# Delta rule and gated MLP on one core: GpSimd's tensor_tensor replaced, zero products tied to the first solve, weight loads paced, new ranks

## Chip, cores, metric

One core of a Trainium2 chip. The metric is the device time of one execution in microseconds, less is better.

## What is computed

The reference runs a delta rule over 4 x 8 heads of 768 steps with head size 48, and puts its output through an MLP with w_in (384 x 2048) and w_out (2048 x 384), both float64 in memory:

```
k_n = k / (norm(k) + 1e-06)
for t in range(S):
    y[t] = einsum('bhd,bhde->bhe', q[t], state)
    v_old = einsum('bhde,bhd->bhe', state, k_n[t])
    state = state + beta[t] * einsum('bhd,bhe->bhde', k_n[t], v[t] - v_old)
x = y.transpose(0, 2, 1, 3).reshape(B * S, H * D)
h = x @ w_in
g = h * tanh(log1p(exp(h)))
out = g @ w_out
```

## The kernel before

The 768 steps are cut into 12 chunks of 64 steps. All 32 heads of a chunk are worked on together. Within a chunk the recurrence is a triangular system. Its solution is made for two chunks at a time, in a group g (`early`, L496): k is turned (kt), products pg give the inner products of k, `diagonal` and `beside` (L534, L539) bring the blocks out of PSUM, `first_block` (L548) masks one of them on GpSimd, VectorE transposes (gt, L564), normalizes (L577 to L604) and eliminates column by column (`step`, L638, the pairs of lines L643 and L644). For the first two groups the elimination is of 16 columns, and `merge` (L676) joins the halves by products ma (L686) and mb (L697), an addition (L702) and a transpose tn (L705). Products ta and tb (`s_a2`, `s_b2`) complete the inverse.

A chunk then goes through `s_gq` (products of k and the state with k and q), `s_z` (pz), `s_y` (py for the output, ps for the new state), each for two halves h of the heads. `turn` (L1017) transposes the output into x, as a high and a low part. v is scaled by the norms first (`scale_v`, L866: eight ScalarE instructions a half for chunk 0, one GpSimd tensor_tensor a half after that, L876), and gq waits for it.

`moe(n)` (L1036) is the MLP on the 256 rows of chunk n, in eight steps fp: up (h, 18 products), Mish and a cast on ScalarE (L1070, L1071), a subtraction for the low part (L1073, on VectorE, but on GpSimd for steps 6 to 15 counted from the start, by GP0 = 6), and down (acc, 12 products).

The weights come as pairs of 32-bit words, 28 pieces (`parts`: three of w_in, four of w_out, four times over). `load_w` issues their loads on SP, one after another. `convert` (L391) makes two float32 parts of each: a copy on ScalarE (L415), a clamp (L426, on GpSimd or, for every fourth piece, on VectorE), a sign (L423 on GpSimd or L421 on VectorE), two joins on VectorE (L430), the high part on ScalarE (L442), and the low part by products with an identity (loi, loo, L447 and L449) for the first 25 pieces.

The order of every engine's instructions is made while the program is built: `Plan` keeps a list of operations with an engine, a cost and a priority, and runs them in a simulated time; the constants SOON to GQ2 near the end are these ranks. The planner also models how TensorE's instructions arrive (`feed`). Where it finds TensorE idle during the first 220 us it puts in products of zeros (`fill_up`, L101, `fill`, L479), which write to a spare PSUM tile named warm.

## Time and profile before

| what | us |
|---|---|
| median of three runs | 639.32 (639.23 to 641.89) |
| the profiled execution | 637.26 |
| its span | 635.5 |
| TensorE busy | 605.9 (95%) |
| VectorE busy | 447.7 (70%) |
| ScalarE busy | 277.3 (44%) |
| GpSimd busy | 157.3 (25%) |

Busy time is an average over very different stretches: the first solve, the conversion of the weights with the first chunk, the second solve, and a steady stretch from there to the end. The span is the profiled execution's from its first to its last instruction; 1.8 us of its time lie around it.

### The profile page before, as it was taken

Reading aid. Unit: us, or ns where it says so; the run is one execution under the profiler, and the core shown is the slowest. Engines: PE = TensorE matmul, PEld = TensorE weight load, DVE = VectorE, ACT = ScalarE, POOL = GpSimd, SP = SyncE. Lnnn points to the kernel's source line nnn. Section 1 sums busy time; section 2 is a strip of 40 time slices with the busy share of each in tenths; the row PEclk is TensorE's granted clock in tenths of the full one; section 3 lists DMA queues with packets and bytes.
Section 4 is the critical chain, followed back from the end, with each engine's and each line's share of the span. In section 5 each row is a group of like instructions: output and inputs, shape, how many; then the busy total and the mean of one; then the engine's idle time right before and its main releaser. Section 6 shows DMA issues by size and latency. Waiting matters only on the chain.

```text
span 635.5 us, 21881 instructions
## 1 busy us (share of the span) xinstructions
PE 605.9 (95%) x9536; PEld 552.8 (87%) x9536; DVE 447.7 (70%) x954; ACT 277.3 (44%) x602; POOL 157.3 (25%) x156
## 2 busy tenths in 40 slices
PE   6888999995899999999999999999999999999997
PEld 3446787894899999999999999999999999999997
DVE  4856889998147999587999569996789994631110
ACT  1725887531354333545224643236543326443331
POOL 5494779751314110103111012101031110000000
PEclk9878999996899999999999999999999999999999
DMA  7997342001324121342213351105131220110011
GB/s 109 387 399 122 53 64 53 2 1 36 44 38 68 39 39 27 51 76 37 45 24 51 44 85 40 26 14 77 34 47 38 40 44 10 27 27 1 1 26 25
DMA packets 156256, 37.70 MB, mean 59 GB/s; under 512 B 149504, under 2 KB 152576, under 8 KB 156160
## 3 DMA queue, kind: packets, MB, share of 16 engines
q1 hardware_dynamic: 151040, 35.80, 27.9%
q8 instruction: 75, 1.23, 0.8%
q10 hardware_dynamic: 5120, 0.49, 0.6%
q14 instruction: 21, 0.17, 0.1%
HBM read 31.56 MB, written 4.72 MB: 57 GB/s over the span
## 4 chain that ended last, share of the span: by engine, by line
PE 71%; DVE 18%; DMA 5%; issue 2%; ACT 2%; POOL 1%; SPq 1%; DVEq 0%; ACTq 0%; POOLq 0%
PE acc L1063 26%; PE h L1053 25%; PE py L719 3%; DMA ri<-in_moe_w_in_dram 3%; DVE pr L643 3%; DVE gt L644 3%; PE gq L719 2%; PE pg L521 2%; DVE gt L564 2%; PE pz L719 2%; PE ps L719 1%; PE tb L719 1%; PE loo L447 1%; PE xt L1028 1%; PE loi L447 1%
## 5 line engine op out<-in xcount | busy, mean ns | idle before, releaser
L1053 PE MATMUL h<-x,wi 128*128 128x256 f32 x1728 | 226.8, 286 | 1.2 <-issue 1.2
L1063 PE MATMUL acc<-wo,g 128*128 128x384 f32 x1152 | 221.8, 342 | 0.0
L1053 PEld LDWEIGHTS h<-x,wi 128*128 128x128 f32 x1728 | 215.8, 190 | 4.6 <-issue 1.5
L1063 PEld LDWEIGHTS acc<-wo,g 128*128 128x128 f32 x1152 | 200.1, 189 | 2.5
L1073 DVE TENSOR_TENSOR g<-e,g 128x512 fp32r<-128x512 f32 x86 | 64.7, 756 | 95.5 <-ACT g L1071 95.2
L1070 ACT ACTIVATE e<-h 128x512 f32<-128x512 f32 x96 | 57.3, 597 | 163.6 <-DVE g L1073 69.0
L1071 ACT CAST g<-e 128x512 fp32r<-128x512 f32 x96 | 59.4, 619 | 65.6 <-PE acc L1063 64.5
L644 DVE TENSOR_TENSOR gt<-gt,pr 128x84 f32<-128x84 f32 (+14 forms) x148 | 53.2, 359 | 5.1
L643 DVE TENSOR_TENSOR pr<-gt 128x84 f32<-128x84 f32 (+14 forms) x148 | 52.8, 357 | 3.2
L550 POOL TENSOR_TENSOR d<-at,lmask 32x512 f32<-32x512 f32 x20 | 27.5, 1375 | 99.7 <-DVE d L536 62.2
L931 DVE TENSOR_TENSOR xx<-gq,amask 64x256 f32<-64x256 f32 x96 | 40.5, 422 | 2.1
L674 POOL COPY tt<-tt 32x512 f32<-32x512 f32 x24 | 16.7, 698 | 93.7 <-DVE tt L657 88.2
L924 DVE TENSOR_TENSOR vt<-vt,gq 64x192 f32<-64x192 f32 (+1 forms) x66 | 23.2, 352 | 22.8 <-PE gq L719 21.8
L876 POOL TENSOR_TENSOR vt<-vt,ne 128x384 f32<-128x384 f32 x22 | 20.0, 927 | 66.8 <-PE h L1053 42.5
L719 PE MATMUL gq<-xx,kt 64*64 64x112 f32 (+1 forms) x768 | 31.3, 261 | 1.3 <-DVE xx L884 1.3
L743 ACT COPY xx<-pz 64x192 f32<-64x192 f32 x92 | 28.7, 312 | 7.0 <-PE pz L719 4.8
L997 DVE TENSOR_TENSOR xx<-xx,ps 48x192 f32<-48x192 f32 x80 | 28.2, 352 | 4.9 <-PE ps L719 3.5
L719 PEld LDWEIGHTS py<-xx 128*64 128x64 f32 x768 | 25.2, 142 | 5.5 <-issue 3.5
L884 DVE STREAM_TRANSPOSE xx<-qsrc 64x512 f32<-64x512 f32 x40 | 28.2, 706 | 1.2
L719 PE MATMUL pz<-vt,tt 64*64 64x48 f32 x768 | 27.6, 218 | 1.1 <-ACT tt L743 1.1
L719 PE MATMUL py<-xx 128*64 128x48 f32 x768 | 28.0, 228 | 0.0
L719 PEld LDWEIGHTS pz<-vt,tt 64*64 64x64 f32 x768 | 22.6, 133 | 5.8 <-issue 1.8
(149 smaller groups left out, 668.5 us busy)
## 6 DMA issues: line engine op xcount, KB each, us to landing
ri<-in_moe_w_in_dram SPq DMA_DIRECT2D x12, 512.0 KB, 9.3
ro<-in_moe_w_out_dram SPq DMA_DIRECT2D x16, 384.0 KB, 9.0
vt<-in_v_dram SPq DMA_DIRECT2D x24, 192.0 KB, 4.2
xx<-in_k_dram SPq DMA_DIRECT2D x48, 96.0 KB, 2.9
out_dram<-o SPq DMA_DIRECT2D x48, 96.0 KB, 2.2
ksrc<-in_k_dram SPq DMA_DIRECT2D x44, 64.0 KB, 2.7
qsrc<-in_q_dram SPq DMA_DIRECT2D x40, 64.0 KB, 2.6
ksrc<-in_k_dram SPq DMA_DIRECT2D x44, 32.0 KB, 2.6
```

The lines of the kernel that those rows point to most:

```text
L643: nc.vector.tensor_tensor(out=pv, in0=nj, in1=xj, op=ALU.mult)
L644: return nc.vector.tensor_tensor(out=below, in0=below, in1=pv, op=ALU.add).ins
L719: last = nc.tensor.matmul(*a, start=True, stop=True)
L743: (nc.scalar.copy if e == "ACT" else nc.vector.tensor_copy)(out=a, in_=b)
L884: nc.vector.transpose(xx[h][r, :, hh, D:D + C], src)
L931: nc.vector.tensor_tensor(out=x[r, p4, hh, D:D + C], in0=pg[h4]()[i, :, d:], in1=bcast_mid(amask[i], 4), op=ALU.mult)
L997: nc.vector.tensor_tensor(out=old, in0=old, in1=ps[h4]()[i], op=ALU.add)
L1053: nc.tensor.matmul(h()[:, f2, :], wt["i", f * P // WI * NCH + c][:, i2, f0:f0 + P], x[:, c, :], start=(i == 0), stop=(i == 3 * NCH - 1))
L1063: nc.tensor.matmul(acc[t]()[:, :DM], gg()[:, a, f2, ts_], wt["o", f][:, i2, :], start=(f == 0 and i == 0), stop=(f == NF - 1 and i == 2))
L1070: m = op("ACT", 0.58, prio + 0.1, lambda e=e, h=h: nc.scalar.activation(e(), h(), AF.Mish, scale=-1.0), m, bufs=[h, e])
L1071: m = op("ACT", 0.58, prio + 0.1, lambda e=e, gg=gg: nc.scalar.copy(out=gg()[:, 0], in_=e()), m, bufs=[e, gg])
L1073: m = op(on, 0.72 if on == "DVE" else 1.32, prio + 0.1, lambda e=e, gg=gg, on=on: (nc.vector if on == "DVE" else nc.gpsimd).tensor_tensor( ...
```

## The change

- `first_block` becomes an affine_select on the same data; `scale_v` becomes eight tensor_scalar of 48 columns a half; the subtraction L1073 is always on VectorE. With that GpSimd runs no tensor_tensor.
- `fill_up`, `fill` and their bookkeeping go. A function `zeros` ties one product of zeros to each of the steps 4, 6, 8, 10 and 12 of the first elimination, and one each behind ma and mb of chunk 0, without a wait.
- 140 products of 16 x 16 (BURN) stand behind the turn of q of chunk 0.
- gq of chunk 0 no longer waits for the scaled v; its second half comes after ma.
- From the tenth piece on, the load of piece k waits for ScalarE's copy of piece k - 8 (PACE = 8).
- All clamps are on GpSimd (CLAMP_POOL); the ranks have other values.

```
+        if EW < k - PACE:
+            tc.add_manual_dep(d.ins, marks[copied[k - PACE]].name, SYNC, reason="as fast as they are used")
...
+        def scaled():
+            marks[copied[k]] = nc.scalar.activation(a(), words()[:, :, 1].bitcast(F32), AF.Copy, scale=2.0 ** -112).ins
+        copied[k] = o = op("ACT", 0.16 + 0.46 * u, prio, scaled, got, bufs=held)
+        if EW < k < len(parts) - PACE:
+            loads[k + PACE].after.append(o)
...
+    def zeros(o, gated=True, n=1, few=False):
+        f = o.fn
+        def marked():
+            marks[o] = f()
+        def products():
+            for i in range(n):
+                r = slice(32 * (i % 4), 32 * (i % 4) + 16)
+                x = identr.bitcast(BF16)[r, 0:16]
+                p = nc.tensor.matmul(warm()[r, 0:16], x, x, start=True, stop=True) if few else nc.tensor.matmul(
+                    warm(), ident, zcol.broadcast_to([P, 512]), start=True, stop=True)
+                if i == 0 and gated:
+                    tc.add_manual_dep(p.ins, marks[o].name, SYNC, reason="not before")
...
-                    nc.gpsimd.tensor_tensor(out=dt()[r, t2], in0=am()[r], in1=bcast_mid(lmask[r], NP), op=ALU.mult)
+                    nc.gpsimd.affine_select(out=dt()[r, t2], in_=am()[r], pattern=[[0, NP], [1, 32]], compare_op=ALU.is_ge, fill=0.0,
+                                            base=0, channel_multiplier=-1)
...
+            if g == 0 and j in (4, 6, 8, 10, 12):
+                zeros(o)
...
         o = mas[n] = op("PE", 1.1, at(0.0), ma, u, bufs=[dt, tu, ps], words=256)
+        if n == 0:
+            zeros(o, gated=False)
...
-        vdn[n, h] = op("POOL", 0.9, prio, lambda: nc.gpsimd.tensor_tensor(
-            out=vt(), in0=vt(), in1=bcast_in(ne()[:, n16:n16 + PB], D), op=ALU.mult), ned[n // 2], *after, bufs=[vt.base, ne])
+        def scaled():
+            for p in range(PB):
+                nc.gpsimd.tensor_scalar(vt()[:, p, :], vt()[:, p, :], ne()[:, n16 + p:n16 + p + 1], None, op0=ALU.mult)
+        vdn[n, h] = op("POOL", 2.0, prio, scaled, ned[n // 2], *after, bufs=[vt.base, ne])
...
+        if n == 0 and h == 1:
+            zeros(m, gated=False, n=BURN, few=True)
...
-        return Stage(0.95, 64, products, [*qdn[n, h], ktd[n], vdn[n, h], *sdn.get((n - 1, h), ())], [kt, *pg], outs)
+        return Stage(0.95, 64, products, [*qdn[n, h], ktd[n], *((vdn[n, h],) if n else ()), *sdn.get((n - 1, h), ())], [kt, *pg], outs)
...
-            on = "POOL" if GP0 <= NFP * n + fp < 2 * NFP else "DVE"
...
-    SOON, SOON1, E1, EG, ES, LATE1, LATE = -0.04, 1.451, 0.508, -0.827, 1.373, 0.174, 0.334
-    E1S, LAG, PRIO_XT, CV0, CV1, G1A, XA, GQ2 = 0.229, 3.048, 0.354, -0.48, 1.221, 1.108, 0.272, 0.985
+    SOON, SOON1, E1, EG, ES, LATE1, LATE = -0.047, 1.599, 0.631, -0.653, 1.608, 0.025, 0.334
+    E1S, LAG, PRIO_XT, CV0, CV1, G1A, XA, GQ2 = 0.401, 3.048, 0.578, -0.521, 1.221, 1.108, 0.203, 1.132
-    KW, EW, GP0, TQ = 10, 0, 6, 2
+    KW, EW, BURN, TQ, PACE = 8, 0, 140, 2, 8
-    CLAMP_POOL = [k for k in range(len(parts)) if k % 4 < 3]
+    CLAMP_POOL = [k for k in range(len(parts)) if k % 4 < 6]
...
-        issue(-89.5 + 0.1 * h, s_gq(0, h))
+        m = issue(-89.5 + 0.1 * h, s_gq(0, h))
+    m.after.append(mas[0])
```

How the order moves, at three places. On TensorE, in the first solve: before, from the last record of gq to ta of chunk 0 (warm<-zcol are zeros, loi belongs to a weight).

```order
L719 MATMUL gq_11_469<-xx_81,kt_145 64x64 x2
L482 MATMUL warm<-zcol,identr 128x512 x7
L686 MATMUL ma_558<-tu_529,d_216 32x16 x64
L482 MATMUL warm<-zcol,identr 128x512 x2
L697 MATMUL mb_641<-tt_82,ym_229 32x16 x64
L447 MATMUL loi_713<-mi_390,identr 128x512
L449 MATMUL loi_713<-wi_707,identr 128x512
L447 MATMUL loi_721<-mi_464,identr 128x512
L449 MATMUL loi_721<-wi_719,identr 128x512
L719 MATMUL ta_733<-tt_82,at_217 64x64 x16
```

The same place with the change, from the last record of gq's first half; gq_10 and gq_11 are the second half.

```order
L716 MATMUL gq_01_554<-xx_80,kt_145 64x64 x2
L472 MATMUL warm<-zcol,identr 128x512 x5
L679 MATMUL ma_655<-tu_650,d_216 32x16 x64
L472 MATMUL warm<-zcol,identr 128x512
L716 MATMUL gq_10_735<-xx_81,kt_145 64x64 x2
L716 MATMUL gq_11_736<-xx_81,kt_145 64x64 x2
...
L692 MATMUL mb_763<-tt_82,ym_229 32x16 x64
L472 MATMUL warm<-zcol,identr 128x512
L716 MATMUL ta_840<-tt_82,at_217 64x64 x16
```

The second half of gq moved behind ma, and four weight products that stood between mb and ta now stand behind ta.

On GpSimd, at the second solve (group 1: chunks 2 and 3), before: d are the masks, vt the scaling of v, g the subtractions.

```order
L550 TENSOR_TENSOR d_1764<-at_1852,lmask 32x512 x2
L1073 TENSOR_TENSOR g_6_1970<-e_6_1923,g_6_1970 128x512
L569 MEMSET gt_1974 128x16x16
L570 MEMSET d_1764 128x32x16
L1073 TENSOR_TENSOR g_7_2029<-e_7_1988,g_7_2029 128x512
L876 TENSOR_TENSOR vt_892<-vt_892,ne_2070 128x384 x2
L1073 TENSOR_TENSOR g_0_2072<-e_0_2044,g_0_2072 128x512
L876 TENSOR_TENSOR vt_1623<-vt_1623,ne_2070 128x384 x2
```

With the change:

```order
L408 TENSOR_SCALAR solved<-solved 128x384
L540 AFFINE_SELECT d_1966<-at_1967 32x512 x2
L540 AFFINE_SELECT d_1966<-at_2060 32x512 x2
L560 MEMSET gt_2160 128x16x16
L561 MEMSET d_1966 128x32x16
L875 TENSOR_SCALAR vt_958<-vt_958,ne_2263 128x48 x16
L875 TENSOR_SCALAR vt_1806<-vt_1806,ne_2263 128x48 x16
L654 MEMSET ym_2466 128x32x16
```

The subtractions left GpSimd, and 32 small instructions stand where four stood.

On VectorE, the last rows ahead of the second solve (gt<-d is its transpose), with the change:

```order
L526 TENSOR_TENSOR d_1966<-pg_0_2026,lmask 128x256
L435 SCALAR_TENSOR_TENSOR wo_2108<-solved,wo_2108 128x384
L526 TENSOR_TENSOR d_1966<-pg_1_2029,lmask 64x256 x2
L1072 TENSOR_TENSOR g_5_1972<-e_5_1907,g_5_1972 128x512
L1072 TENSOR_TENSOR g_6_2105<-e_6_2020,g_6_2105 128x512
L884 STREAM_TRANSPOSE xx_81<-qsrc 64x8x64 x2
L1072 TENSOR_TENSOR g_7_2154<-e_7_2130,g_7_2154 128x512
L555 STREAM_TRANSPOSE gt_2160<-d_1966 128x1024
```

Before, g_6 and g_7 were on GpSimd, the transpose of q (xx<-qsrc) came after the solve, and the solve followed g_5 and a weight.

## Rows read from the trace of the kernel before

**Rows 1.** The page, DMA queues (packets, MB, share) and issues (KB each, us to landing).
```profile
q8 instruction: 75, 1.23, 0.8%
...
ri<-in_moe_w_in_dram SPq DMA_DIRECT2D x12, 512.0 KB, 9.3
```
**Rows 2.** Stretches: start:end, length, busy us of each engine, granted clock, DMA share, GB/s.
```profile
63.00:142.60 79.60, 78.04 (x1187) 65.95 (x1185) 71.08 (x123) 55.54 (x120) 59.49 (x45) 1.00 0.23 35
...
151.00:161.00 10.00, 10.00 (x348) 9.45 (x350) 6.73 (x11) 1.72 (x4) 1.76 (x2) 0.69 0.25 36
...
215.00:600.00 385.00, 383.43 (x5664) 367.79 (x5663) 287.13 (x631) 159.76 (x343) 42.44 (x47) 1.00 0.23 38
```
**Rows 3.** Timeline of TensorE, 0 to 66 us: start, us, what, [idle before, releaser].
```profile
28.13 6.64 PE L482 MATMUL warm<-zcol,identr 128*128 128x512 f32 x14 [0.77 <-ACT mi L415]
34.70 1.26 PE L686 MATMUL ma<-tu,d 16*32 16x16 f32 x128
...
41.14 1.26 PE L697 MATMUL mb<-tt,ym 32*32 32x16 f32 x80 [2.74 <-issue]
...
46.89 1.61 PE L719 MATMUL ta<-tt,at 32*64 32x64 f32 x32
...
62.94 2.29 PE L1053 MATMUL h<-x,wi 128*128 128x256 f32 x18
```
**Rows 4.** Timeline of VectorE, 0 to 66 us.
```profile
19.39 0.21 DVE L644 TENSOR_TENSOR gt<-gt,pr 128x28 f32<-128x28 f32 x1
...
24.28 0.55 DVE L643 TENSOR_TENSOR pr<-gt 128x100 f32<-128x100 f32 x1
24.87 0.26 DVE L644 TENSOR_TENSOR gt<-gt,pr 128x100 f32<-128x100 f32 x1
...
28.32 1.15 DVE L655 STREAM_TRANSPOSE tu<-gt 128x512 f32<-128x512 f32 x1
...
31.12 3.50 DVE L931 TENSOR_TENSOR xx<-gq,amask 64x256 f32<-64x256 f32 x8
...
42.46 0.42 DVE L702 TENSOR_TENSOR tt<-tt,mb 128x256 f32<-128x256 f32 x1 [4.63 <-PE mb L697]
```
**Rows 5.** Timeline of GpSimd, 0 to 66 us.
```profile
24.01 2.02 POOL L426 TENSOR_SCALAR mi<-mi 128x512 f32<-128x512 f32 x1 [7.35 <-ACT mi L415]
26.11 1.54 POOL L423 TENSOR_SCALAR ri<-mi 128x512 f32<-128x512 f32 x1
...
36.78 1.20 POOL L423 TENSOR_SCALAR ro<-mo 128x384 f32<-128x384 f32 x1
...
42.94 1.73 POOL L674 COPY tt<-tt 32x512 f32<-32x512 f32 x2 [0.77 <-DMA ri<-in_moe_w_in_dram]
```
**Rows 6.** Timeline of VectorE, 66 to 166 us.
```profile
121.80 1.63 DVE L453 SCALAR_TENSOR_TENSOR wo<-spare,wo 128x384 fp32r<-128x384 f32 x1
...
128.22 2.12 DVE L564 STREAM_TRANSPOSE gt<-d 128x1024 f32<-128x1024 f32 x1
...
131.25 1.22 DVE L590 TENSOR_SCALAR y<-ss 128x32 int32<-128x32 int32 x1
...
137.23 0.86 DVE L644 TENSOR_TENSOR gt<-gt,pr 128x28 f32<-128x28 f32 x1
...
141.75 1.23 DVE L643 TENSOR_TENSOR pr<-gt 128x88 f32<-128x88 f32 x1
...
149.78 1.06 DVE L655 STREAM_TRANSPOSE tu<-gt 128x512 f32<-128x512 f32 x1
```
**Rows 7.** Timeline of GpSimd, 66 to 166 us.
```profile
117.04 5.97 POOL L550 TENSOR_TENSOR d<-at,lmask 32x512 f32<-32x512 f32 x4
```
**Rows 8.** Timeline of TensorE, 110 to 200 us.
```profile
150.90 1.90 PE L686 MATMUL ma<-tu,d 16*32 16x16 f32 x128 [8.10 <-DVE tu L655]
...
158.17 2.38 PE L1063 MATMUL acc<-wo,g 128*128 128x384 f32 x12
...
167.21 3.92 PE L1063 MATMUL acc<-wo,g 128*128 128x384 f32 x12
```

## Prediction before the change was run

> **What bounds the kernel now.** I read the table of stretches first [rows 2]. From 215 to 600 us TensorE is busy for 383.43 of 385 us at the full clock, and VectorE for three quarters of that; work moved between GpSimd and VectorE there can't shorten anything, it can only do harm. So the time is decided by how soon the steady stretch begins, and the landmark that I use is the first down product of the second chunk (acc, at 158.17) [rows 8]: the products that stand before it are the same in both programs, apart from zeros. Then I read TensorE's timeline up to 63 us, where the first up product (h) starts at 62.94 [rows 3], and VectorE's and GpSimd's beside it [rows 4, 5]. The reader is to see that the solve is over on VectorE at 29.47 (tu, 28.32 + 1.15) while TensorE works off zeros until 34.77, and that mb stands still for 2.74 us in the middle of its 128 products, waiting for nothing that the profile shows. In the page the instruction queue has its own traffic beside the weights [rows 1], so I take this stop for late instructions. Between 63 and 142.6 us TensorE has 78.04 of 79.6 us of work [rows 2]. Then it stands idle for 8.10 us until VectorE's second solve is done (tu, 149.78 + 1.06) [rows 6, 8], and the next 10 us run at a granted clock of 0.69.
>
> **The first solve: zeros and tiny products.** Before, 14 records of zeros (28.13 to 34.77) stand between gq and ma [rows 3]. The change puts five zero products behind gq of the first half, each held back until a step of the solve (steps 4 to 12) is done; the last of these steps is past before tu. At 0.46 us a record (6.64/14) five products of two records are 4.6 us; gq now starts when its copies are there, not after the scaling of v, so they end at about 29.5, with tu. ma then starts at about 29.6 instead of 34.70 and takes 1.26. Behind it come one zero product (0.92), the second half of gq (0.6) and mb (1.26): mb is over at about 33.7, unless it is short of instructions. The 140 tiny products stand in the idle time before gq. They use up instructions there, so that the next ones are fetched in that gap and mb has its own by then. Their price: ma's 128 take 1.26 us, so about 1.4 us; by the 80 of mb behind its stop, also 1.26 us, it would be 2.2. Either is hidden by the wait for the copies.
>
> VectorE can't add mb earlier than its own queue allows: the eight masks (31.12 + 3.50) and one join of a weight (about 0.7) come first, so the addition is at 35.3 instead of 42.46 [rows 4]: 7.1 us. After the addition (0.42) and the transpose (0.71) TensorE took ta only at 46.89, 3.3 us later, since it had four slow weight products in front [rows 3]; now ta stands right behind mb, which gives 3.2 back. From ta to the first h it was 16.05 us. There the order of the pieces is nearly the same: ma of the second chunk (1.26) now stands ahead of h, and the copy of the diagonal blocks on GpSimd (42.94, needed by the copies of tb) comes after one more clamp. By GpSimd's chain from 24.01 [rows 5] it would start at about 41, which is when tb is done, so it costs 0 to 1.7 us; the first two thirds of these 16 us ran at a low clock and may run faster. I set the rest at nothing. **Sum of this part: −10.3 us**, the first h at 52.6. Bounds: −6 (TensorE falls to the low clock, its short products double) to −12.
>
> **Weights loaded as they are used.** From the tenth piece on a load waits on SP for ScalarE's copy of the piece eight before. Behind a waiting load stand, on SP, loads of k and v of the next chunks. GpSimd needs some 3 us for a piece (2.02 + 1.54 for a large one [rows 5], less for a small one), so a load has some 25 us, against a landing time of 9.3 us with all weights in flight [rows 1]. I cost it at nothing. What it takes away is the crowd on the DMA engines while ma and mb fetch their instructions; this is part of the term above. If the cover is gone, each late piece costs the whole landing time.
>
> **The conversions.** All 28 clamps go to GpSimd: 7 more, at most 2.02 us each, 14 us; the two halves of v of the second chunk become 16 small tensor_scalar. A tensor_scalar with one operation takes 1.54 us at 512 columns and 1.20 at 384 [rows 5]; the line through both gives 0.31 at 48 columns. Bounds: 0.1 (columns alone) to 1.20. So 5.0 us instead of two tensor_tensor. GpSimd gets about 17 us more beside TensorE's 79.6 us stretch, in which it works 59.49 us [rows 2]: 77, nearly full. It has been ahead of TensorE until now; with TensorE 10 us earlier it may fall behind. I take **+2.5 us**, between 0 and +8. VectorE loses seven clamps, on which nothing hangs.
>
> **The second solve.** Here tensor_tensor on GpSimd stops VectorE. While four of them run (117.04, 1.49 us each) [rows 7], a step of VectorE that needs 0.56 takes 1.63 (121.80) [rows 6], three times over; and the six steps from 137.23 to 142.98 take 5.58 us, where the same six took 1.34 from 19.39 on [rows 4, 6]. With three more before them (1.7 us in all; the worst took 1.22 at 131.25 [rows 6]) the solve lost 6.0 us, of 22.6 from 128.22 to tu's end at 150.84. A tensor_scalar costs VectorE much less: beside one of 2.02 us a step took 0.55, the next of its shape 0.26 [rows 4, 5]. That is 0.29 for 512 columns, or 0.03 for 48. During the new solve 32 such run on GpSimd: 1.0 us. So it takes 17.7 us.
>
> The Trainium skill says otherwise (SBUF — State Buffer, Who interferes with whom): a VectorE instruction with two SBUF inputs contends with any GpSimd instruction that reads SBUF, and the loser is blocked for the whole instruction. The trace agrees for tensor_tensor (1.63 us) and not for tensor_scalar (0.55 beside 2.02). By that page the solve would gain nothing, and the sum would be that of the first rival below.
>
> The two subtractions for g_6 and g_7 move to VectorE ahead of the solve (0.7 each). It starts 2.0 us later in TensorE's work than before: 130.2 on the old clock, tu's end at 147.9. TensorE has h_3 of the second chunk as well before ma, so its work reaches to 142.6 + 2.2 = 144.8, and it idles 3.1 us instead of 8.1. Two ma (2.5) and VectorE's second transpose (1.87) with g_0 (0.7) end together at about 150.5; acc is there then instead of at 158.17 [rows 8]: **−7.6 us**. Bounds: −9.5 (no idle time) to +1 (the first rival). Afterwards acc at 167.21 took 3.92 us [rows 8], 1.6 above its usual 2.3, at a low clock; after a shorter idle time I expect it at the full one: **−1.6 us**, or 0.
>
> **The rest costs nothing.** The ten subtractions that go to VectorE (7 us in all) and the 16 small instructions per chunk in place of two lie beside TensorE, which is full. The masks of the first block (affine_select, 32x512) have no row of their size; I take the 1.49 of the tensor_tensor that they replace [rows 7] and allow for nothing as for twice that. The last of these ended at 123.01 and the solve began at 128.22, so 5 us cover them. Other ranks only exchange neighbours.
>
> **Sum:** −10.3 + 2.5 − 7.6 − 1.6 = −17.0, on the profiled execution's 637.26: 620.3. The median of the runs is 639.32, 2.1 above it; I predict 622.0 for a median.
>
> **Rivals.**
> 1. *GpSimd's small instructions hold VectorE for their whole length.* Then 32 times 0.31 = 9.9 us replace the 6.0 in the second solve: it takes 26.5 us, and the term −7.6 becomes about +1, the −1.6 goes. −10.3 + 2.5 + 1 = −6.8: 632. For it: tensor_tensor does so, and the page. Against it: the 0.55 beside 2.02.
> 2. *The front doesn't hold.* mb still lacks instructions or runs at the low clock, since fewer zeros keep TensorE awake; or conversions on GpSimd eat what was won. The −10.3 becomes −5, or +2.5 becomes +8: 627.5. For it: GpSimd at 77 of 79.6 us. Against: the zeros that went stood in the way more than they helped.
> 3. *Slower: the small tensor_scalar are dear.* In the steady stretch VectorE has a quarter free [rows 2], some 20 us per two chunks, in which 32 small ones run while it solves. From 0.6 us each, held in full, they use that up, and VectorE is the bound. At the 1.20 of a 384-column one: 38 us per two chunks, less 10 for the tensor_tensor that are gone, less 20 free: +8 in each of four later pairs, and +16 in the second solve: 637 + 32 + 16 − 8, about 677. At 0.7 it is about 645. Against it: the line at 0.31.
> 4. *Nothing changes:* TensorE's stretch to 142.6 stretches by what the front wins, because something else times it (GpSimd's copies and ScalarE's queue): 638.
>
> **How the numbers follow.** Forecast 0.62, its own bounds 613 to 629; rival 1 0.13, rival 2 0.13, rival 3 0.07, rival 4 0.05. The range 612 to 633 takes in rivals 1 and 2 and leaves out 0.12 and the tails of the bounds. A measurement of this kernel can tell 0.5% (3.2 us) from no change: faster is below 636.1, the forecast with rivals 1 and 2: 0.88; within 0.05; slower 0.07.
>
> **What would show it.** Right: ma at about 30 and mb without a stop; the first h near 53; VectorE's steps of the second solve at 0.2 to 0.3 us throughout; idle time before ma of the second solve of 3 us; acc of the second chunk near 143 (158 − 10 + 2.5 − 7.6); 215 to 600 as full as before. Wrong: steps of 0.5 and more beside small tensor_scalar (rival 1); a stop inside ma, mb or ta, or a clock under 0.9 from 30 to 53 us (rival 2); TensorE waiting for loi or loo products with GpSimd busy without a gap (rival 2); idle time on TensorE after 215 us with VectorE full (rival 3).

## The result and the profile after

The changed kernel takes 630.77 us (median of 4, 629.34 to 631.29), the kernel before 639.28 beside it: 0.9856 of the time, 95% interval 0.9824 to 0.9887. The change is faster by 8.5 us, where 17.3 were forecast. The profiled execution took 630.43 us, its span is 628.7 (before 635.5).

The page of the kernel after: GpSimd's two new groups (busy us, mean ns of one | idle before) and the weight loads' landing, 6.4 us instead of 9.3 [rows 1].

```profile
L875 POOL TENSOR_SCALAR vt<-vt,ne 128x48 f32<-128x48 f32 x176 | 79.2, 474 | 69.8 <-DVE gt L635 48.2
...
L540 POOL TENSOR_SCALAR_AFFINE_SELECT d<-at 32x512 f32<-32x512 f32 x20 | 14.7, 734 | 101.1 <-ACT at L531 100.5
...
ri<-in_moe_w_in_dram SPq DMA_DIRECT2D x12, 512.0 KB, 6.4
```

The same stretches as [rows 2], after (the granted clock is the third figure from the end; 1.00 is the upper level of 2.4 GHz, 0.50 the lower of 1.2 GHz):

```profile
63.00:142.60 79.60, 78.81 (x1197) 66.90 (x1197) 68.02 (x131) 56.77 (x122) 62.55 (x59) 1.00 0.43 93
151.00:161.00 10.00, 8.61 (x308) 8.00 (x301) 5.52 (x13) 2.88 (x6) 1.76 (x4) 0.61 0.02 5
215.00:600.00 385.00, 384.37 (x5684) 369.18 (x5683) 273.27 (x614) 161.35 (x345) 72.54 (x143) 1.00 0.23 38
```

Where the time went is seen best by landmarks, the start of a down product (acc) in TensorE's timeline. The two profiled executions are 6.8 us apart (637.26 and 630.43), so they account for that much of the 8.5:

| landmark | before | after | difference |
|---|---|---|---|
| first acc of chunk 0 | 92.42 | 90.15 | -2.3 |
| first acc of chunk 1 | 158.17 | 154.70 | -3.5 |
| first acc of chunk 2 | 215.01 | 210.67 | -4.3 |
| first acc of chunk 11 | 605.55 | 598.35 | -7.2 |
| span | 635.5 | 628.7 | -6.8 |

The first of these landmarks needs care. Before, 32 products of gq and 32 of pz stand ahead of the first acc of chunk 0 and take 1.4 us there (91.03 to 92.42); with the change they stand behind it. So 1.4 of its 2.3 us are only order, and the front brought some 0.9 us, where 10 were forecast. The first h, by which the prediction reckoned its front, even comes 2.5 us later than before (65.42 against 62.94), with one ma (1.26) now ahead of it. At the other landmarks the products ahead are the same apart from zeros and tiny ones. From the front to the first acc of chunk 2 the change brought some 3.4 us, where 9 were forecast for the second solve and the clock behind it, and 2.9 us came from the steady stretch, where nothing was forecast.

**The front.** TensorE's timeline after, from the tiny products to the first h, to be held against [rows 3]:

```profile
18.00 1.26 PE L472 MATMUL warm<-identr 16*16 16x16 bf16 x140
19.19 0.39 PE L716 MATMUL gq<-xx,kt 64*64 64x64 f32 x3
24.23 1.12 PE L716 MATMUL gq<-xx,kt 64*64 64x64 f32 x29 [4.65 <-issue]
25.29 6.44 PE L472 MATMUL warm<-zcol,identr 128*128 128x512 f32 x10
31.66 0.93 PE L679 MATMUL ma<-tu,d 16*32 16x16 f32 x89
35.45 0.51 PE L679 MATMUL ma<-tu,d 16*32 16x16 f32 x39 [2.87 <-issue]
35.90 2.08 PE L472 MATMUL warm<-zcol,identr 128*128 128x512 f32 x2
...
38.97 0.76 PE L692 MATMUL mb<-tt,ym 32*32 32x16 f32 x53
42.24 0.93 PE L692 MATMUL mb<-tt,ym 32*32 32x16 f32 x75 [2.52 <-issue]
...
45.10 1.97 PE L716 MATMUL ta<-tt,at 32*64 32x64 f32 x32
...
65.42 4.43 PE L1055 MATMUL h<-x,wi 128*128 128x256 f32 x36
```

Three stops for nothing that the profile shows (4.65, 2.87 and 2.52 us), where before there was one of 2.74 [rows 3]. A zero record takes 0.64 and later 1.04 us instead of 0.46: the granted clock is 0.59 from 25 to 30 us, 0.66 from 35 to 40 and 0.50 from 45 to 55.

**The second solve.** VectorE and TensorE around it, after:

```profile
130.86 2.06 DVE L555 STREAM_TRANSPOSE gt<-d 128x1024 f32<-128x1024 f32 x1
...
141.15 0.34 DVE L635 TENSOR_TENSOR gt<-gt,pr 128x100 f32<-128x100 f32 x1
...
148.31 1.07 DVE L648 STREAM_TRANSPOSE tu<-gt 128x512 f32<-128x512 f32 x1
```

```profile
149.52 3.46 PE L679 MATMUL ma<-tu,d 16*32 16x16 f32 x242 [5.24 <-DVE tu L648]
154.37 0.41 PE L679 MATMUL ma<-tu,d 16*32 16x16 f32 x14 [1.39 <-issue]
154.70 4.21 PE L1065 MATMUL acc<-wo,g 128*128 128x384 f32 x12
...
164.12 2.38 PE L1065 MATMUL acc<-wo,g 128*128 128x384 f32 x12
```

From gt to the end of tu the solve takes 18.52 us instead of 22.62 [rows 6]; no step of the elimination is longer than 0.35. But it starts at 130.86, later than before, so TensorE idles 5.24 us, then stops in ma, and it is now the first acc that runs at the low clock.

**The steady stretch.** Before, TensorE had a stop in gq in every second chunk (223.9, 313.0, 402.5 and 491.5 us), released by VectorE's transpose of q. First the group in the page, then two lines of TensorE, three of VectorE and one of GpSimd, before:

```profile
L719 PE MATMUL gq<-xx,kt 64*64 64x112 f32 (+1 forms) x768 | 31.3, 261 | 1.3 <-DVE xx L884 1.3
```

```profile
223.78 0.37 PE L719 MATMUL gq<-xx,kt 64*64 64x112 f32 x2
224.48 0.32 PE L719 MATMUL gq<-xx,kt 64*64 64x112 f32 x3 [0.33 <-DVE xx L884]
```

```profile
214.94 0.81 DVE L643 TENSOR_TENSOR pr<-gt 128x30 f32<-128x30 f32 x1
215.79 0.78 DVE L644 TENSOR_TENSOR gt<-gt,pr 128x30 f32<-128x30 f32 x1
...
222.98 1.44 DVE L884 STREAM_TRANSPOSE xx<-qsrc 64x512 f32<-64x512 f32 x2
```

```profile
214.59 1.90 POOL L876 TENSOR_TENSOR vt<-vt,ne 128x384 f32<-128x384 f32 x2
```

After, there is none. Between the first acc of chunk 2 and the fifth of chunk 11, gq and pz take 22.9 us of TensorE's time instead of 26.2 (from the start of each record to the start of the next); the stretch became 2.9 us shorter.

### The profile page after: what moved, and what is told of

It reads as the page before. It is cut to its first block, busy times and chain, and to the rows that moved or that the text cites. A ratio compares the mean times of both kernels' runs of the same rounds, so it can differ in the third digit from the quotient of the medians.

```text
span 628.7 us, 22302 instructions
## 1 busy us (share of the span) xinstructions
PE 600.8 (96%) x9660; PEld 552.2 (88%) x9660; DVE 436.6 (69%) x957; ACT 278.1 (44%) x602; POOL 203.0 (32%) x307
## 3 DMA queue, kind: packets, MB, share of 16 engines
q8 instruction: 76, 1.25, 0.9%
## 4 chain that ended last, share of the span: by engine, by line
PE 86%; DVE 6%; issue 3%; POOL 2%; DMA 1%; ACT 0%; SPq 0%; POOLq 0%; DVEq 0%; ACTq 0%
PE h L1055 31%; PE acc L1065 31%; PE py L716 4%; PE gq L716 3%; PE pz L716 2%; PE warm L472 2%; PE loi L429 2%; PE ps L716 2%; PE tb L716 2%; PE ta L716 1%; PE pg L511 1%; PE xt L1030 1%; PE ma L679 1%; PE loo L429 1%; PE qt L897 1%
## 5 line engine op out<-in xcount | busy, mean ns | idle before, releaser
L1055 PE MATMUL h<-x,wi 128*128 128x256 f32 x1728 | 222.8, 284 | 1.9 <-issue 1.9
L1055 PEld LDWEIGHTS h<-x,wi 128*128 128x128 f32 x1728 | 213.2, 188 | 5.9 <-issue 2.2
L1072 DVE TENSOR_TENSOR g<-e,g 128x512 fp32r<-128x512 f32 x96 | 69.4, 726 | 108.7 <-ACT g L1071 108.4
L875 POOL TENSOR_SCALAR vt<-vt,ne 128x48 f32<-128x48 f32 x176 | 79.2, 474 | 69.8 <-DVE gt L635 48.2
L635 DVE TENSOR_TENSOR gt<-gt,pr 128x84 f32<-128x84 f32 (+14 forms) x148 | 48.9, 330 | 5.1
L634 DVE TENSOR_TENSOR pr<-gt 128x84 f32<-128x84 f32 (+14 forms) x148 | 46.9, 317 | 3.3
L540 POOL TENSOR_SCALAR_AFFINE_SELECT d<-at 32x512 f32<-32x512 f32 x20 | 14.7, 734 | 101.1 <-ACT at L531 100.5
L667 POOL COPY tt<-tt 32x512 f32<-32x512 f32 x24 | 17.3, 722 | 64.3 <-DVE tt L650 47.7
L716 PEld LDWEIGHTS gq<-xx,kt 64*64 64x64 f32 x768 | 20.8, 141 | 7.3 <-DVE gt L635 4.7
```

The lines of the kernel that those rows point to most:

```text
L634: nc.vector.tensor_tensor(out=pv, in0=nj, in1=xj, op=ALU.mult)
L635: return nc.vector.tensor_tensor(out=below, in0=below, in1=pv, op=ALU.add).ins
L716: last = nc.tensor.matmul(*a, start=True, stop=True)
L875: nc.gpsimd.tensor_scalar(vt()[:, p, :], vt()[:, p, :], ne()[:, n16 + p:n16 + p + 1], None, op0=ALU.mult)
L1055: nc.tensor.matmul(h()[:, f2, :], wt["i", f * P // WI * NCH + c][:, i2, f0:f0 + P], x[:, c, :], start=(i == 0), stop=(i == 3 * NCH - 1))
L1072: m = op("DVE", 0.72, prio + 0.1, lambda e=e, gg=gg: nc.vector.tensor_tensor(out=gg()[:, 1], in0=e(), in1=gg()[:, 0], op=ALU.subtract), m, ...
```

## Where TensorE's instructions come from

This reading carries the experiments on the front. Counting TensorE's own instructions in order of start (products, weight loads, semaphore instructions), the three stops lie ahead of numbers 961, 1217 and 1473: 256 apart. Before, the stop in mb is ahead of number 1217 as well. In the fourteen profiles of this study (before, after and twelve runs) 67 stops of over 0.3 us between 15 and 300 us have no releaser, and all 67 lie at such a number (193 more than a multiple of 256). The queue q8, of the kind named instruction, carries packets of 16 KB (1.25 MB in 76), about one for each 256. The view of DMA packets after, from 24.4 us to ma's stop at 32.6, then the instruction queue in the 1.7 us behind that and from 39.8 to 41, while mb stands:

```profile
DMA packets 3485, 1.83 MB, mean 223 GB/s; under 512 B 3176, under 2 KB 3176, under 8 KB 3484
...
q8 instruction: 1, 0.02, 5.6%
...
q8 instruction: 1, 0.02, 5.3%
```

No such packet runs from 24.4 to 32.6 us; one starts at 32.65 and takes 1.51, and ma goes on at 35.45, 1.29 after its end. The next starts at 39.85, takes 1.01, and mb goes on 1.38 after its end. Behind all the stops that lie at these numbers TensorE goes on 1.2 to 1.8 us after the end of the packet that it lacked. In the steady stretch a packet mostly starts within 1.3 us of TensorE entering the block before the one it brings; in this run, between 17 and 45 us, it took 3.0 to 8.4 us. ma and mb (128 products each, every one with its weight load) use up a block of 256 in 1.26 us, so no fetch of that length hides beside them.

The Trainium skill (Runtime: NRT & Kernel Launch, Instruction fetch mechanics) has the same blocks of 256 instructions on a DMA queue of their own, and calls the cost of crossing a boundary "mostly hidden". The trace agrees on the blocks; where TensorE stopped in ma or mb of the first solve, the crossings cost 1.4 to 6.4 us each.

## Experiments

Two theories of the front stood against each other: *delivery* (the stops come at the ends of packets that start late) and the prediction's own idea (the tiny products spare ma and mb their stop). For the second solve the question was whether tensor_tensor on GpSimd had been its price.

**Without the tiny products.**

```
-            for i in range(n):
+            for i in range(0 if few else n):
```

> The changed kernel without its 140 tiny products; the order of everything else is the same. Delivery theory (TensorE's instructions come in packets of 16 KB, 256 instructions each, two of them held at a time; a packet that is asked for while loads fill the DMA engines starts 3 to 8 us late): with 280 instructions fewer ahead of it the packet that ends in ma is asked for before gq and is there in time, so ma runs through; the next one is asked for in ma and mb still stops, after about 67 of its 128 products, for 2 to 4 us. First h 2 to 4 us earlier than 65.4, time 627 to 630 against 630.8. The prediction's own idea (the tiny products spare ma and mb their stop): without them the stops get longer, first h later, time 631 to 634. Rival (where the packets end doesn't matter): stops of the same sum, 5 us, time within 1 us of 630.8.

0.9862 of before (0.9825 to 0.9899), 628.2 us. TensorE's timeline of this run:

```profile
31.22 1.25 PE L679 MATMUL ma<-tu,d 16*32 16x16 f32 x128 [2.24 <-DVE tu L648]
...
35.47 0.86 PE L692 MATMUL mb<-tt,ym 32*32 32x16 f32 x65
38.06 0.71 PE L692 MATMUL mb<-tt,ym 32*32 32x16 f32 x63 [1.74 <-issue]
...
59.91 4.43 PE L1055 MATMUL h<-x,wi 128*128 128x256 f32 x36
```

ma runs through, mb stops after 65 products, again ahead of instruction 1217; the stop in gq is gone, and the first h comes 5.5 us earlier than with the change, more than the 2 to 4 expected. The time as a whole is not clear of the change's own (0.9824 to 0.9887). Delivery holds: the tiny products did use up instructions, and so brought a packet's end into ma.

**Quiet DMA engines.** All loads from the eighth piece on, and q, k and v of the next chunk, wait for the addition behind mb.

```
+            if n == 1:
+                tc.add_manual_dep(d.ins, marks["add", 0].name, SYNC, reason="after mb")
...
+        if k == HOLD:
+            tc.add_manual_dep(d.ins, marks["add", 0].name, SYNC, reason="after mb")
...
+    HOLD = 7
...
+        if k == HOLD:
+            got[k].after.append(last_s["sum", 0])
...
+        if n == 1:
+            after.append(last_s["sum", 0])
```

> The changed kernel, with all loads from the eighth weight piece on (and q, k, v of the next chunks) held back until the addition behind mb. The DMA engines then have little to do from about 29 to 40 us. Delivery theory: the packets for ma and mb start within about 2 us of being asked for; ma has no stop, that of mb is at most 1.5 us (as the 1.39 and 1.26 us later on, with the DMA engines quiet); mb ends at 37.5 to 40 rather than 43.2. What that is worth in the end is open, since the weights come later: first h 60 to 66, time 626 to 636. Rival (the packets are late because they are asked for late, the crowd has no part in it): ma stops for 2.9 and mb for 2.5 us as before, and the time is longer by what the late weights cost.

1.0013 (0.9991 to 1.0035). Half a hit:

```profile
30.15 0.93 PE L683 MATMUL ma<-tu,d 16*32 16x16 f32 x89
33.27 0.60 PE L683 MATMUL ma<-tu,d 16*32 16x16 f32 x39 [2.19 <-issue]
...
35.80 2.17 PE L696 MATMUL mb<-tt,ym 32*32 32x16 f32 x128
```

mb runs through and ends at 38.0. But ma still stops, though no packet at all was under way from 26 us on: the packet that it lacked started at 30.92, 0.8 us after ma had begun and 7.3 after TensorE had entered the block before (8.4 with the change); for mb it was 1.7 (4.4). So the crowd explains part of the lateness, not all of it; when a packet is asked for while TensorE stands at a semaphore stayed open. What the front won (first h at 61.80) is lost behind it: the first acc of chunk 1 comes at 164.78, 10 us later than with the change. That late weights did it is not shown: behind mb no engine waits for a weight's load, and the hold also gave the planner another order on VectorE and TensorE.

**Each half of the change alone.** The kernel before without tensor_tensor on GpSimd (affine_select, tensor_scalar, GP0 = 99):

```
-                    nc.gpsimd.tensor_tensor(out=dt()[r, t2], in0=am()[r], in1=bcast_mid(lmask[r], NP), op=ALU.mult)
+                    nc.gpsimd.affine_select(out=dt()[r, t2], in_=am()[r], ...)
...
-        vdn[n, h] = op("POOL", 0.9, prio, lambda: nc.gpsimd.tensor_tensor(
...
+        def scaled():
+            for p in range(PB):
+                nc.gpsimd.tensor_scalar(vt()[:, p, :], vt()[:, p, :], ne()[:, n16 + p:n16 + p + 1], None, op0=ALU.mult)
...
+        vdn[n, h] = op("POOL", 2.0, prio, scaled, ned[n // 2], *after, bufs=[vt.base, ne])
...
-    KW, EW, GP0, TQ = 10, 0, 6, 2
+    KW, EW, GP0, TQ = 10, 0, 99, 2
```

> The kernel before with one part of the change: no tensor_tensor on GpSimd (masks as affine_select, v by eight tensor_scalar, all subtractions on VectorE). Theory: the second solve (transpose gt to the end of tu) goes from 22.6 to 18 to 19 us, its steps stay under 0.4 us, TensorE's idle time before ma goes from 8.1 to 3 to 6 us; the stops of 0.59 us in gq of the steady stretch stay, since they come from the order. Time 639.3 to 634 to 636. Rival (small GpSimd instructions hold VectorE as long): solve 22 us or more, time 638 to 641. Rival (the whole gain of the change comes from here): 630 to 632.

0.9962 (0.9939 to 0.9985), 635.22 us. The solve went from 22.62 to 18.03 us, as expected, and TensorE's idle time before ma to 2.65. Yet chunk 2 came no earlier: its first acc stands at 215.39 us (215.01 before). The first acc of chunk 0 was 2.2 us later in this run (94.59, with the same products ahead), and ma of the second solve now stops for 2.17 us; the rest is not shown. So in this profile the shorter solve was worth nothing by itself. The stops in gq were to stay, and they went: VectorE's order in the steady stretch is as before, but the transposes of q come at 220.94 instead of 222.98 us and gq never waits. In the old order these stops thus came from tensor_tensor holding VectorE; this alone is 3.4 us from chunk 2 to chunk 11, all that the run gained. The new ranks remove them as well: in the two runs that follow, with tensor_tensor on GpSimd in the new order, gq does not wait either (gq and pz take 22.9 us in both, as with the change).

The other half, the changed kernel with all three tensor_tensor back on GpSimd:

```
-                    nc.gpsimd.affine_select(out=dt()[r, t2], in_=am()[r], ...)
+                    nc.gpsimd.tensor_tensor(out=dt()[r, t2], in0=am()[r], in1=bcast_mid(lmask[r], NP), op=ALU.mult)
...
-        vdn[n, h] = op("POOL", 2.0, prio, scaled, ned[n // 2], *after, bufs=[vt.base, ne])
+        vdn[n, h] = op("POOL", 0.9, prio, lambda: nc.gpsimd.tensor_tensor(
...
+            on = "POOL" if 6 <= NFP * n + fp < 2 * NFP else "DVE"
```

> The changed kernel with all three tensor_tensor back on GpSimd (masks, scaling of v, ten subtractions): the front, the paced loads and the ranks alone. Theory: the first solve and its front are as with the whole change (first down product 1 to 3 us earlier than before, with stops in ma and mb); the second solve takes 21 to 23 us again. Time 634 to 637, so that this part and the run without tensor_tensor (2.4 us) together give what the change gives, 8.5 us. Rival (the two parts need each other): 638 or more.

1.0005 (0.998 to 1.003), and the rival hit: 2.4 and 0 us alone, 8.5 together. In this run's order the solve with tensor_tensor begins at 133.27, 2.4 us later than with the change, and takes 23.56 us, 5.0 longer; GpSimd has five subtractions beside it:

```profile
133.03 1.30 POOL L1069 TENSOR_TENSOR g<-e,g 128x512 fp32r<-128x512 f32 x1 [2.19 <-ACT g L1067]
...
146.60 2.53 POOL L1069 TENSOR_TENSOR g<-e,g 128x512 fp32r<-128x512 f32 x2
```

The first acc of chunk 2 comes at 217.85 us, 7.2 later than with the change, about the sum of the two. Why the solve begins later is not shown: with other costs for these operations the planner's order changed from 67 us on.

**v by tensor_tensor again**, all else as changed:

```
-            for p in range(PB):
-                nc.gpsimd.tensor_scalar(vt()[:, p, :], ...)
+            nc.gpsimd.tensor_tensor(out=vt(), in0=vt(), in1=bcast_in(ne()[:, n16:n16 + PB], D), op=ALU.mult)
```

> The changed kernel with one part undone: v is scaled by one tensor_tensor a half again, in place of eight tensor_scalar; the order is the same. Theory: in the second solve four tensor_tensor hold VectorE, steps of 0.8 to 1.2 us appear beside them, the solve takes 21 to 23 us instead of 18.5, TensorE's idle time before ma 8 to 9.5 instead of 5.2; the steady stretch doesn't change. Time 633 to 635 against 630.8. Rival (the solve got shorter because the subtractions were moved ahead of it): solve within 1 us of 18.5, time within 1 us.

0.9907 (0.9876 to 0.9939), not clear of the change's own interval. A miss in size: the solve takes 19.60 us, 1.1 more than with the change, four steps are over 0.5 (at most 0.86), and TensorE idles 6.32 us before ma, not 8 to 9.5. With the run above this puts, by difference, some 4 of the 5 us on the subtractions and 1 on the scaling of v. The rest of the loss in this run's profile lies in longer stops (ma 3.98) and a longer low clock, which vary from run to run.

**The pacing**, undone as a whole:

```
-        if EW < k - PACE:
-            tc.add_manual_dep(d.ins, marks[copied[k - PACE]].name, SYNC, reason="as fast as they are used")
...
-        if EW < k < len(parts) - PACE:
-            loads[k + PACE].after.append(o)
```

> The changed kernel without the pacing of the weight loads. Theory (the DMA engines are as full of small pieces of q, k and v as of weights, so pacing takes little away): stops in ma and mb within 1 us of 2.87 and 2.52, the landing time of the weights back to 9 us, time within 2 us of 630.8. Rival (the pacing shortens the stops): stops of 4 us and more, time 633 to 636. Rival (the paced loads come late for GpSimd): 627 to 629.

1.0028 (1.0009 to 1.0048): all 8.5 us are gone, and none of the three expectations named the reason. The first h comes at 65.35, as with the change; ma stops 5.11 us, mb 1.62. The loss is in the second solve, where TensorE waits for a subtraction in VectorE's queue:

```profile
143.59 0.62 PE L1061 MATMUL acc<-wo,g 128*128 128x384 f32 x2
151.43 3.57 PE L1061 MATMUL acc<-wo,g 128*128 128x384 f32 x10 [7.22 <-DVE g L1068]
```

In this program all weight loads stand on SP ahead of k, q and v of the next chunk (41 to 57 us instead of 21 to 43), and the planner orders the conversions and the solve around that. To tell order from waits, the waits alone were taken out:

```
-        if EW < k - PACE:
-            tc.add_manual_dep(d.ins, marks[copied[k - PACE]].name, SYNC, reason="as fast as they are used")
```

> The changed kernel with the order of the paced loads, but without their waits: on every engine the same instructions in the same order, and a load is issued as soon as SP comes to it. The unpaced run lost 9 us, and there the order on SP was another too (k, q and v of the next chunks behind all weights). Theory (the order did it, the waits do little): time within 2 us of 630.2. Rival (the waits keep the DMA engines freer, for TensorE's instructions among others): stops in ma and mb of 4 us and more, time 634 or more.

0.9886 (0.9857 to 0.9915), as the changed kernel in its second comparison (0.9889, below), though the median, 632.93 us, is 2.7 above the 630.2. The stop in ma is 6.38 us, the size that the rival named, but with the waits it was 2.87 once and 5.64 once. The order is worth 9 us, the waits nothing that can be told.

**Zeros to keep the clock up**, two in place of the tiny products and nine tied ones instead of five:

```
-            if g == 0 and j in (4, 6, 8, 10, 12):
+            if g == 0 and j in (1, 3, 4, 6, 8, 9, 10, 12, 13):
...
-            zeros(m, gated=False, n=BURN, few=True)
+            zeros(m, gated=False, n=2)
```

> As the run without tiny products, but with two zero products in their place and nine tied zero products instead of five, so that TensorE has something to do from the turn of q to ma. Clock theory: the granted clock is at its upper level from 20 to 36 us (0.6 to 0.7 in the changed kernel), a zero record takes 0.46 instead of 0.64 us, ma starts with the end of tu; mb still stops for 1.5 to 3 us at a packet's end. If the clock stays up over this stop, ta, tb and pz take 1.2 to 1.4 us each instead of 1.97 and the first h comes at 54 to 57 instead of 59.9: 624 to 627. Rival (the stop in mb lowers the clock anyway, as in the kernel before at 40 to 45 us): first h at 58 to 60, time within 1 us of the run without tiny products. Rival (the zeros still run at the low clock and push ma behind tu): first h after 62, 630 or more.

0.9853 (0.9833 to 0.9873), 628.47 us. A miss: the first h comes at 63.97 us, 4 later than without the tiny products (59.91), where the theory had 54 to 57 and its first rival 58 to 60; the second had it after 62, but a time of 630 or more.

```profile
19.35 0.69 PE L716 MATMUL gq<-xx,kt 64*64 64x64 f32 x32
...
26.16 4.61 PE L472 MATMUL warm<-zcol,identr 128*128 128x512 f32 x10 [0.40 <-DVE gt L635]
...
34.33 1.32 PE L716 MATMUL gq<-xx,kt 64*64 64x64 f32 x32
35.57 0.93 PE L692 MATMUL mb<-tt,ym 32*32 32x16 f32 x53
40.28 1.25 PE L692 MATMUL mb<-tt,ym 32*32 32x16 f32 x75 [3.78 <-issue]
...
43.46 1.97 PE L716 MATMUL ta<-tt,at 32*64 32x64 f32 x32
```

A zero record takes 0.46 us again: the granted clock is 1.00 from 17.6 to 34.6 us. From 34.7 to 55.1 it is 0.50, and so ta takes 1.97 us as with the change. But the fall comes ahead of mb's stop (36.5 to 40.28): gq's second half, before that stop, takes 1.32 us where its first half took 0.69. So it is not this stop that lowered the clock. Ahead of the fall TensorE had stood 1.32 us before ma, then done ma and one zero product; what lowered it is not shown.

**The changed kernel once more**, beside the last runs:

> The changed kernel itself, on the same chip as the other three, for comparison: 0.983 to 0.988 of the time of the kernel before; stops in gq, ma and mb at the same instructions as in its first profile (961, 1217 and 1473 of TensorE's own count).

0.9889 (0.9864 to 0.9914), stops ahead of 961, 1217 and 1473 as before. The one in ma was 5.64 us instead of 2.87, and the first acc came at 92.03. In the run without the paced waits, which has the same order, it was 6.38. So one and the same stop varies by 3.5 us from run to run; the first h of these three varies by 1.9 (65.42, 67.27 and 65.75).

**Without the zero behind ma** (and without tiny products):

```
         o = mas[n] = op("PE", 1.1, at(0.0), ma, u, bufs=[dt, tu, ps], words=256)
         if n == 0:
-            zeros(o, gated=False)
+            zeros(o, gated=False, some=False)
```

> As the run without tiny products, with the zero product behind ma taken out as well, all else in the same order; in that run its two records took 2.07 us between ma and mb. Delivery theory: mb starts 2 us earlier and stops 2 us earlier, after about 67 products, but goes on at the same time as before, since the packet is asked for in ma and comes when it comes (38.06 in that run): mb's stop is 3 to 4 us instead of 1.7, first h within 0.7 us of 59.9, time within 1 us of 628.2. Rival (the work between ma and mb is what counts): stop of 1.7 us, first h 1.5 to 2 us earlier, 626.

0.9813 (0.9799 to 0.9828), 627.93 us.

```profile
34.22 1.12 PE L716 MATMUL gq<-xx,kt 64*64 64x64 f32 x28 [0.97 <-DVE xx L933]
35.27 1.14 PE L692 MATMUL mb<-tt,ym 32*32 32x16 f32 x67
38.54 1.04 PE L692 MATMUL mb<-tt,ym 32*32 32x16 f32 x61 [2.13 <-issue]
```

mb stops after 67 products and goes on at 38.54 (38.06 with the zero). That the time of going on is set by the packet fits delivery; but mb started only 0.2 us earlier, since gq waited for VectorE's masks, so the run doesn't exclude the rival. The first h misses its mark: 61.45 us, where 59.9 within 0.7 was expected, after 17 us at a granted clock of 0.50 (34.3 to 51.3). It is the fastest version of the study against before; its interval overlaps that of the changed kernel by 0.0004 in the first comparison (0.9824 to 0.9887) and lies under it in the second (0.9864 to 0.9914).

**A short hold** of the loads, from the tenth piece on, in the program without tiny products:

```
+        if k == HOLD:
+            tc.add_manual_dep(d.ins, marks["add", 0].name, SYNC, reason="after mb")
...
-            for i in range(n):
+            for i in range(0 if few else n):
...
+    HOLD = 9
...
+        if k == HOLD:
+            got[k].after.append(last_s["sum", 0])
```

> As the run without tiny products, with the weight loads from the tenth piece on held until the addition behind mb; k, q and v of the next chunk are loaded before that as in the changed kernel, and mb now stands ahead of the second half of gq. Delivery theory: the DMA engines are done with the earlier loads at about 30 us, the packet for mb starts within 2 us of being asked for in ma, mb's stop ends by 36.5 instead of 38.1 and is at most 3 us (mb also comes earlier), first h 56 to 60. Since GpSimd waits in its queue for the copy behind mb anyway, the later weights cost it little: 624 to 629. Rival (the weights then come too late, as in the run with quiet DMA engines, 638.8): first h as early, but TensorE or VectorE waits for weights after 60 us, 631 or more.

0.9908 (0.9875 to 0.9942), 633.35 us; the profile is that of the fastest of its six runs (630.93). The front does what delivery says:

```profile
34.02 1.01 PE L694 MATMUL mb<-tt,ym 32*32 32x16 f32 x98
36.39 0.43 PE L694 MATMUL mb<-tt,ym 32*32 32x16 f32 x30 [1.36 <-issue]
...
38.43 1.15 PE L718 MATMUL ta<-tt,at 32*64 32x64 f32 x32
```

mb goes on at 36.39 (36.5 expected), ta runs at the full clock, and the first h comes at 59.24, 6.2 us earlier than with the change. But the second solve begins at 132.07, no earlier than with the change (130.86 and 132.73 in its two profiles), and the first acc of chunk 11 is 0.8 us behind its first profile: what the front won is lost on the way to the solve. The time is the rival's (631 or more), its reason is not shown: behind mb the one wait for a weight's load is ScalarE's, of 0.8 us, and with the hold the planner's order on VectorE and TensorE is another from 35 us on.

**Seven clamps back on VectorE**, on top of the fastest version:

```
-    CLAMP_POOL = [k for k in range(len(parts)) if k % 4 < 6]
+    CLAMP_POOL = [k for k in range(len(parts)) if k % 4 < 3]
```

> As the run without tiny products and without the zero behind ma, with one more part of the change undone: every fourth clamp (7 of 28) is on VectorE again. Theory (GpSimd, busy for 19.4 of every 20 us from 60 to 120 us whenever the front ends, is what times the start of the second solve, so what the front wins is not passed on): GpSimd has about 12 us less, falls under 19 of 20, the last clamp and with it the second solve come 2 to 5 us earlier (solve from 128.75 to 124 to 127), TensorE's idle time before ma gets shorter; time 624 to 627 against 627.9. Rival (the subtractions and transposes on VectorE time the solve): it starts within 1 us of 128.75 or later, time 627.5 to 631.

0.9833 (0.9808 to 0.9858). GpSimd's busy time fell as expected. The same stretch (busy us of TensorE, its weight loads, VectorE, ScalarE, GpSimd), first without and then with this edit:

```profile
80.00:100.00 20.00, 17.74 (x254) 13.31 (x252) 16.96 (x33) 16.30 (x37) 19.39 (x15) 1.00 0.57 102
```

```profile
80.00:100.00 20.00, 18.81 (x317) 14.68 (x316) 16.40 (x32) 16.65 (x37) 13.16 (x11) 1.00 0.77 170
```

The solve began at 131.31 instead of 128.75, not earlier: the theory that GpSimd times it falls, the rival hit. With the clamps the planner's order changed too, so what times the start of the second solve stays open; VectorE works there almost without a gap (11.11 of the 11.70 us before the solve in the run without this edit), and there three subtractions and the transposes of q stand between the last weight and the solve.

## Why the prediction was right and where it was not

The sign and the range (612 to 633) held, and rival 2 ("The front doesn't hold", 627.5) named the largest shortfall. The forecast of 622.0 was 8.8 us off (its terms add up to 622.3), and the landmark, acc of the second chunk, came at 154.70 instead of near 143. By these terms:

- **Front, -10.3: measured about -0.9** with the same products ahead, and +2.5 at the first h, by which it was reckoned (65.42, where 52.6 was forecast). The step that failed: "They use up instructions there, so that the next ones are fetched in that gap and mb has its own by then." The tiny products cost no time of their own, as said (1.26 us, hidden), and brought 280 instructions; they moved a packet's end into ma. Without them ma has no stop. The five zero products were put at 0.46 us a record by a row at the full clock; after the stop in gq they took 0.64, and from 43 us to 56 short products took up to twice their time. The chain up to mb's end: 43.2 instead of 33.7. One reading was wrong too, that the first two thirds of the 16 us from ta to h ran at a low clock before: from 46.89 to 62.94 us the granted clock was 0.50 only up to 47.9 and from 54.8 to 58.1.
- **Paced loads, 0: without their order the whole gain is gone (9 us).** "I cost it at nothing" was right of the waits and wrong of the order on SP that comes with them, which brings k, q and v of the next chunk forward. I looked at what stands behind a waiting load, not at what is now ahead of it.
- **Conversions, +2.5: not to be seen by itself.** With seven clamps back on VectorE the intervals overlap (0.9808 to 0.9858 against 0.9799 to 0.9828). A 48-column instruction took 0.47 us on the mean, not 0.31, with no harm on GpSimd that a run shows. affine_select took 0.73 us, below the 1.49 allowed for. GpSimd is busy for 62.55 of the 79.6 us, not 77: the subtractions and masks by tensor_tensor that leave this stretch were not taken off (4.9 and 5.8 us before; the new masks take 3.3).
- **Second solve, -7.6: measured -2.6** from the front to the first acc of chunk 1 (-3.5 there, less the 0.9). Its mechanism was right and its size nearly: 18.5 us for a forecast of 17.7. The 28 steps take 7.92 us with 23 of the 32 small tensor_scalar beside them, and 7.05 in the first solve of the run of before without tensor_tensor: 0.9 us, where 1.0 was forecast for all 32, so rival 1 (9.9 us) is out. What failed is the start: "It starts 2.0 us later in TensorE's work than before: 130.2 on the old clock" took the front's gain along, and the solve started at 130.86 on the new one. The front's gain reached the solve in one run (without tiny products: first acc 4.0 us earlier than with the change, solve 3.7) and not in another (short hold: first h 6.2 us earlier, solve 1.2 later). And the run of before without tensor_tensor had the shorter solve and no earlier chunk 2: the two gains are not independent, as the sum took them to be.
- **Low clock, -1.6: measured about 0.** The acc at 164.12 takes 2.38, but the one at 154.70 takes 4.21.
- **Steady stretch, 0: measured -2.9.** "Work moved between GpSimd and VectorE there can't shorten anything" read TensorE's 383.43 of 385 us as full. A record's end is modelled, and a gq that takes 0.59 us from its start to the next showed an idle time of 0.33; the page had a sign of it (1.3 us before gq, released by the transpose of q) in one row. Either half of the change ends these stops by itself. The rows of VectorE behind it would have shown steps of 0.81 beside tensor_tensor.

On the small instructions the rule of the Trainium skill that was weighed ahead (SBUF — State Buffer, Who interferes with whom) would have let each block VectorE for its whole length, by estimate 15 us for 32 at the measured 0.47 us. The trace agrees for tensor_tensor on GpSimd and not for tensor_scalar: 0.9 us.

## What to carry to other kernels

Where an engine issues hundreds of tiny instructions in a microsecond (256 in 1.26 us here), count its instructions from stop to stop: a constant distance says that delivery is the limit, and then fewer instructions ahead of the critical piece help, and padding only moves the stop. A planner's dependency has two effects, the wait and the new order of everything around it; test them apart. A landmark can be compared only where the same work stands ahead of it. And what the front wins counts only if the engine that decides the next meeting point starts earlier too.

## What was not expected of the hardware

- TensorE's stops lie 256 of its instructions apart, and end 1.2 to 1.8 us after the end of a 16 KB packet; in ma of the second solve, with the DMA engines nearly empty, they still took 1.1 to 2.2 us, in the crowded front up to 6.4.
- Behind mb's stop of 2.5 and 2.7 us the two profiles of the changed kernel ran 13.6 us at a granted clock of 0.50 (42.8 to 56.4 and 44.4 to 58.0; ta took 1.97 us). Behind one of 2.74 us the kernel before ran 6.7 us so (41.2 to 47.9), and with the zeros the clock fell before the stop. After a stop of 1.36 us (short hold) ta took 1.15, and the clock was 0.50 only from 42.1 to 48.8.
- Two tensor_tensor on GpSimd (0.83 us or more each) went with two steps of VectorE of 0.8 us where such a one takes about 0.2; eight tensor_scalar on data of the same size went with steps longer by about 0.06 (0.33 instead of 0.27 or 0.28 us at 112 columns).
